# MLP kernel on one core: tile 1's last four blocks turned by DVE, tile 2's late cells moved behind rows 4 to 7's first piece, two centring steps on Pool

## The chip, the cores and the metric

The kernel runs on one core of a Trainium2 chip, in one launch. The metric is the device time in microseconds (us). Unless another thing is said, times inside the kernel are counted from the start of the profiled execution's span.

## The reference

The input x has 2048 tokens of 1024 channels, in bf16. Each token is normalized over its channels and goes through two matrix products with a gelu between.

```python
def _layernorm(x, axis=-1, eps=1e-5):
    m = jnp.mean(x, axis=axis, keepdims=True)
    v = jnp.var(x, axis=axis, keepdims=True)
    return (x - m) / jnp.sqrt(v + eps)

def reference(x, w1, b1, w2, b2):              # x (1, 2048, 1024), w1 (1024, 3584), w2 (3584, 1024)
    y = _layernorm(x, axis=-1)
    h = _gelu(jnp.einsum("bsd,df->bsf", y, w1) + b1)
    return jnp.einsum("bsf,fd->bsd", h, w2) + b2
```

## The kernel before

**Tiling.** A tile is 128 tokens, a block of tokens is four tiles (512), and there are four blocks. A row is 128 of the 3584 columns of w1, so there are 28 rows. For the first product TensorE needs tokens transposed, with channels on the partitions: `yT_sb`, eight channel blocks of 128 (index `dt`, or `j`). A full matmul takes one row and one channel block against 512 tokens. Per block of tokens, the 28 rows of the first product (eight matmuls each, `mm1_row`, L370) go through gelu on ScalarE (ACT, L396) into `hT_sb`; then the second product runs over 28 row blocks for each of four tiles and two halves of the output (`out_chunk`, L438), VectorE (DVE) adds b2 (L449), and SP stores.

**The start of block 0.** While the weights are still arriving, TensorE already works. Tiles 0, 1 and 2 (`RAW`) enter the first product untouched, as raw x, and the normalization is applied afterwards to the sums. Rows 0 to 7 (the wave) are cut into cells: a cell is one row and one channel block for some of the tiles (`wave_cell`, `pe_wave`, L386). w1 for these rows comes in pieces of 128 or 256 KB (`PIECES`): rows 0 to 3 with channel blocks 0, 1, 2-3, 4-5, 6-7 (loads w0 to w4), then rows 4 to 7 with blocks 0-1, 2-3, 4-5, 6-7 (w5 to w8). The tiles of x are loads x0 to x3. SP issues the loads in the order of `SP_FIRST_LOADS` (b1 and w0 go through ACT's queue).

**How raw tiles are turned.** TensorE transposes a 128 x 128 block into PSUM (`pe_T_one`, L331), and ACT copies it from there (`put_copy`, L343). For channel blocks 4 to 7 of tile 2 it is done in another way: DVE transposes 32 x 32 squares within each quarter of the partitions into `xq_sb` (`turn_2`, L492), and 16 small copies put the squares in their places, eight on Pool (L505) and eight on ACT (L509). Their events are `tup2` and `tua2`. Tile 3 is normalized on DVE first (L268) and turned in the same manner, whole (L479, moves at L484, L487, L516).

**Statistics.** DVE makes the statistics of a tile (L254, L264), Pool raises the variance to the power -1/2 (L261, event `rstd<i>`). DVE turns means and powers of tiles 0 to 2 into rows (L469), ACT spreads them over the partitions (L475) as `row_b(0)` and `row_b(1)`.

**Fixes and centring.** For rows 0 to 7 the raw sums are mended by DVE in PSUM: L545 subtracts the mean times the column sum of w1, L548 multiplies by the power; then gelu. Rows 8 to 27 of block 0 use centred tokens instead: four centring steps (`ops_centre`, L538, events `ctr0` to `ctr3`) subtract the mean row from `yT_sb`, two channel blocks and three tiles in each step (128 x 768 elements), into the second buffer of `yT_sb`. Row 8's matmul of channel block `dt` waits for step `dt // 2`. Their power is multiplied in PSUM (L412).

**What sets the order.** Each engine runs a list that the program writes out by hand; waits are on named events. The part of DVE's list that matters here is

```python
seq = st[0] + st[1][:1] + turn_2() + st[1][1:] + st[2] + turn_m[:2] + st[3] + turn_m[2:] + nm[3] + moves_3() + turn_r + ctr[:2]
...
for o in [a0, a1, b0, b1_] + ctr[2:] + [o for f in fixes[2:] for o in f]:
```

where `a0, b0, a1, b1_` are the fixes of rows 0 and 1. Pool's list is: the power of tile 0, tile 2's eight moves, the powers of tiles 1, 2 and 3, tile 3's moves. TensorE's list in the start is: transposes of tiles 0 and 1; cells of w0 for tile 0, then tile 1; four transposes of tile 2; then w1 for tiles 0 and 1; w0 and w1 for tile 2; w2 for all three; w3 for tiles 0 and 1, then tile 2; and from w4 on all three tiles in each cell (386 columns with two columns of ones that give the column sums). Then tile 3 for rows 0 to 7 (128 columns each), then row 8 and on.

Of the kernel before, what the change touches and what calls it, by code (L numbers as in the profile page):

```python
# [9 lines left out]
I32 = mybir.dt.int32  # L10

LN_EPS = 1e-5
P = 128
# [7 lines left out]
RAW = (0, 1, 2)  # L21
N_WARM = 25
GROUPS = (0, 2, 8)
# [3 lines left out]
N_AHEAD = 6  # L27
N_EARLY = 1
N_PAIR = 3
N_TURN = 4  # L30
POOL_TURNS = tuple((tq, (tq + k) % 4) for k in (1, 2) for tq in range(4))
CENTRE = (0, 2, 4, 6, 8)
DVE_MOVES = ((0, 0), (1, 1), (2, 2))
POOL_MOVES = ((3, 3), (0, 1), (1, 2), (2, 3), (0, 2), (1, 3))
W1_COLS = (512, 1024, 1024)
N_W2_CHUNKS = 4
SP_FIRST_LOADS = ("b1", "x0", "x1", "w0", "x2", "w1", "w2", "w3", "x3", "w4", "w5", "w6", "w7", "w8")
N_ONES = 2
PAD = 64

# [56 lines left out]
def bass_standalone__mixer_channel_mlp__prompt_kernel(  # L97
# [13 lines left out]
    DT = D // P  # L111
# [35 lines left out]
    with ExitStack() as es:  # L147
# [178 lines left out]
        def pe_T_one(i, groups, banks, j):  # L326
            k = next(n for n, g in enumerate(groups[1:]) if j < g)
            first, last = j == groups[k], j + 1 == groups[k + 1]
            waits = ["ident", x_ev[i][0]] + ([bank_read[banks[k]]] if banks[k] in bank_read else []) if first else []
            o = (j - groups[k]) * P  # L330
            pe.op(lambda e: e.transpose(out=bank_of[banks[k]][:, o:o + P], in_=x_sb[:, i, j * P:(j + 1) * P],  # L331
                                        identity=ident[:, :]), waits=waits, sig=(f"tp{i}_{k}" if last else None))
            yT_ev.setdefault(i, [None] * DT)[j] = f"te{i}_{k}"
            pe_t[0] += 0.056

        def put_copy(i, groups, banks, k):
            g0, g1 = groups[k:k + 2]
            bname = banks[k]
            assert banks.count(bname) == 1
            src = bank_of[bname][:, 0:(g1 - g0) * P].bitcast(I32)  # L340
            src = src.rearrange("p (j s) -> p j s", j=g1 - g0)
            dst = yT_sb[:, 0, g0:g1, ycol(i):ycol(i) + P].bitcast(I32)
            act.op(lambda e, dst=dst, src=src: e.copy(out=dst, in_=src), waits=[f"tp{i}_{k}"], sig=f"te{i}_{k}")  # L343
            bank_read[bname] = f"te{i}_{k}"
# [32 lines left out]
        def pe_wave(r, dt, tiles, bank, waits, sig):  # L377
            raw = tiles[0] == 0
            base = raw_at if tiles[0] in RAW else 0
            y0 = ycol(tiles[0]) - (N_ONES if raw else 0)  # L380
            n0 = base + y0 - ycol(RAW[0]) if tiles[0] in RAW else 0
            n1 = n0 + ycol(tiles[-1]) + P - y0
            w = list(waits) + (["onecols"] if raw else []) + [yT_ev[t][dt] for t in tiles]
            w += ["tup2"] if 2 in tiles and dt >= N_TURN else []
            w.append(f"w1c{w1_chunk_of(r, dt)}")
            pe.op(lambda e: e.matmul(  # L386
                unit_bank(bank)[:, n0:n1], lhsT=w1_sb[:, dt, r * P:(r + 1) * P], rhs=yT_sb[:, 0 if tiles[0] in RAW else ybuf(0), dt, y0:y0 + n1 - n0],
                start=(dt == 0 and tiles[0] in (0, 3)), stop=(dt == DT - 1), skip_group_check=True),
                waits=w, sig=sig)
            pe_t[0] += _mm_us(n1 - n0)  # L390
            if sig:
                est[sig] = pe_t[0]
# [80 lines left out]
        def put_row_spread(k, q0, q1):  # L473
            for q in range(q0, q1):
                act.op(lambda e, q=q: e.copy(out=row_b(k)[32 * q:32 * (q + 1)], in_=row_b(k)[0:32]),  # L475
                       waits=[f"row_q{k}"], sig=(f"row_{k}" if q == 3 else None))

        def moves_3():
            res = [(lambda e: e.transpose(out=xq_sb[:, :], in_=x_sb[:, 3, :]), [y_ev[3][-1], "tua2", "tup2"], "xq", 1.07)]  # L479
            for tq, q in POOL_MOVES + DVE_MOVES:  # L480
                src = xq_sb[32 * tq:32 * (tq + 1), :].rearrange("p (j q s) -> p j q s", j=DT, q=4)[:, :, q, :].bitcast(I32)
                dst = yT_sb[32 * q:32 * (q + 1), ybuf(0), :, ycol(3) + 32 * tq:ycol(3) + 32 * (tq + 1)].bitcast(I32)
                if (tq, q) in POOL_MOVES:
                    pool.op(lambda e, src=src, dst=dst: e.tensor_copy(out=dst, in_=src), waits=["xq"],  # L484
                            sig=("tg3" if (tq, q) == POOL_MOVES[-1] else None))
                if (tq, q) in DVE_MOVES:
                    res.append((lambda e, src=src, dst=dst: e.tensor_copy(out=dst, in_=src), ["xq"],  # L487
                                ("tc3" if len(res) == len(DVE_MOVES) else None), 0.2))
            return res

        def turn_2():
            return [(lambda e: e.transpose(out=xq_sb[:, 0:(DT - N_TURN) * P], in_=x_sb[:, 2, N_TURN * P:]),  # L492
                     [x_ev[2][0]], "xq2", 0.64)]

        def put_moves_2(eng):
            todo = POOL_TURNS
            if eng is act:
                todo = [m for m in ((tq, q) for tq in range(4) for q in range(4)) if m not in POOL_TURNS]
            for n, (tq, q) in enumerate(todo):
                src = xq_sb[32 * tq:32 * (tq + 1), 0:(DT - N_TURN) * P]  # L500
                src = src.rearrange("p (j q s) -> p j q s", j=DT - N_TURN, q=4)[:, :, q, :].bitcast(I32)
                dst = yT_sb[32 * q:32 * (q + 1), 0, N_TURN:DT, ycol(2) + 32 * tq:ycol(2) + 32 * (tq + 1)].bitcast(I32)
                sig = "tup2" if eng is pool else "tua2"
                if eng is pool:
                    pool.op(lambda e, src=src, dst=dst: e.tensor_copy(out=dst, in_=src),  # L505
                            waits=["xq2"] + {0: ["rstd0"], 4: ["tup2_0"]}.get(n, []),
                            sig={3: "tup2_0", 7: sig}.get(n))
                else:
                    act.op(lambda e, src=src, dst=dst: e.copy(out=dst, in_=src), waits=["xq2"], sig=(sig if n + 1 == len(todo) else None))  # L509

        def put_moves_3():
            todo = [(tq, q) for tq in range(4) for q in range(4) if (tq, q) not in DVE_MOVES + POOL_MOVES]
# [36 lines left out]
                     [f"fx_a{r}", "row_1"], f"fx_b{r}", 0.42)]  # L549

        st = {0: [op_stats(0, 0), op_stats(0, 1), op_aggr(0)]}
        put_moves_2(pool)
        st.update({i: [op_stats(i, 0), op_stats(i, 1), op_aggr(i)] for i in range(1, TPB)})
        nm = {3: ops_norm(3)}
        turn_m, turn_r = ops_row_turn(0), ops_row_turn(1)
        ctr = ops_centre()
        seq = st[0] + st[1][:1] + turn_2() + st[1][1:] + st[2] + turn_m[:2] + st[3] + turn_m[2:] + nm[3] + moves_3() + turn_r + ctr[:2]
        for o in seq:
            dve_put(o)

        pe_b1()
        put_b1()
        T_BANKS = (("t", "2_0"), ("2_1", "1_4"), ("t", "2_0"))
        for t, j in [(0, j) for j in range(N_AHEAD)] + [(1, j) for j in range(GROUPS[1])] + [
                (0, j) for j in range(N_AHEAD, DT)] + [(1, j) for j in range(GROUPS[1], DT)]:
            pe_T_one(t, GROUPS, T_BANKS[t], j)
        for k in range(2):
            for t in RAW[:2]:
                put_copy(t, GROUPS, T_BANKS[t], k)
        wave = [new_unit() for _ in range(R)]  # L570
        opened = set()

        def wave_cell(r, dt, tiles, sig=None):
            waits = [] if r in opened else wave[r][1]
            opened.add(r)
            pe_wave(r, dt, tiles, wave[r][0], waits, sig)

        cells_of = lambda a, b: [(r, dt) for j0, j1, rows in PIECES[a:b] for dt in range(j0, j1) for r in rows]
        for t in RAW[:2]:
            for r, dt in cells_of(0, N_EARLY):  # L580
                wave_cell(r, dt, (t,))
        G2 = (0, GROUPS[1], N_TURN)
        for j in range(N_TURN):
            pe_T_one(2, G2, T_BANKS[2], j)
        for k in range(2):
            put_copy(2, G2, T_BANKS[2], k)
        put_moves_2(act)
        for j in range(N_TURN, DT):
            yT_ev[2][j] = "tua2"
        put_row_spread(0, 1, 4)  # L590
        for r, dt in cells_of(N_EARLY, N_PAIR - 1):
            wave_cell(r, dt, RAW[:2])
        for r, dt in cells_of(0, N_PAIR - 1):
            wave_cell(r, dt, RAW[2:])
        for r, dt in cells_of(N_PAIR - 1, N_PAIR):
            wave_cell(r, dt, RAW)
        for r, dt in cells_of(N_PAIR, N_PAIR + 1):
            wave_cell(r, dt, RAW[:2])
        for r, dt in cells_of(N_PAIR, N_PAIR + 1):
            wave_cell(r, dt, RAW[2:])  # L600
        cells = cells_of(N_PAIR + 1, len(PIECES))
        for n, (r, dt) in enumerate(cells):
            wave_cell(r, dt, RAW, f"raw_{r}" if dt == DT - 1 else None)
        cs_ev = {}

        def put_cs(c0, c1, src):
# [3 lines left out]
            for r in mine:  # L610
                cs_ev[r] = f"cs{c0}"

        put_cs(0, 4, ps_1[:, 0:4, one0:one0 + 1])
        put_moves_3()
        put_row_spread(1, 1, 3)
# [10 lines left out]
            act_gelu(r, 0, TPB, wave[r][0], f"fx_b{r}", f"g_0_{r}")  # L626
            hT_row[(0, r)] = f"g_0_{r}"
        (a0, b0), (a1, b1_) = fixes[:2]
        for o in [a0, a1, b0, b1_] + ctr[2:] + [o for f in fixes[2:] for o in f]:
            dve_put(o)  # L630
        for t in RAW:
            yT_ev[t] = [f"ctr{k}" for k, (j0, j1) in enumerate(zip(CENTRE[:-1], CENTRE[1:])) for _ in range(j0, j1)]
# [94 lines left out]
```

## Time and profile before

| | us |
|---|---|
| median of 3 runs (lowest, highest) | 396.15 (395.9, 396.18) |
| profiled execution | 396.51 |
| its span, first to last instruction | 395.3 |

The profiled execution's time holds 1.2 us around its span. The granted clock of TensorE is 1.00. In the lines that follow, PE is TensorE's matmul and PEld its weight load, and a name such as L386 is the line of the kernel. A line of the timeline has start, length, engine, line, operation, out<-in, shape and count; several instructions of one kind are merged, so that the length covers all of them, and matmuls overlap each other in their pipeline. A line that begins with a source line gives the shortest, median and longest duration in ns and the first and last start.

### The profile page before, as it was taken

The page shows a single profiled execution, that of the slowest core. Times are in us where ns is not written, and L with a number is a line of the kernel's source. Part 1 is how long each engine was busy: PE and PEld are TensorE (multiplying, and loading weights), DVE is VectorE, ACT ScalarE, POOL GpSimd, SP SyncE. Part 2 cuts the span into 40 slices and gives each one's busy share as a digit, 9 for nine tenths or more (in the row PEclk, how much of TensorE's full clock was granted, in tenths as well). Part 3 has the DMA queues.
Part 4 walks back from the last instruction along what each step waited for, and adds up shares of the span by engine and source line. Part 5 has one row for each costly group of instructions (what it writes and reads, how often), then busy time and mean ns, then how long its engine had stood idle before and what let it go on. Part 6 is the DMA issues. An engine that isn't in the chain of part 4 may idle for free.

```text
span 395.3 us, 4562 instructions
## 1 busy us (share of the span) xinstructions
PE 390.9 (99%) x1916; PEld 185.8 (47%) x1950; DVE 162.7 (41%) x339; ACT 87.1 (22%) x145; POOL 14.0 (4%) x69
## 2 busy tenths in 40 slices
PE   9999999999999999999999999999999999999998
PEld 8744444444444444444444444444444444444444
DVE  6998889998999306987100000001100000001011
ACT  5655420000134332000023443000003334400000
POOL 5201000011001100000000000000000000000000
PEclk9999999999999999999999999999999999999999
DMA  7999930000000000000000000000000000000000
GB/s 273 375 385 387 387 139 27 15 27 14 28 0 0 2 0 0 28 27 15 27 13 2 0 0 2 13 13 28 25 15 15 0 2 0 0 15 27 13 28 27
DMA packets 16078, 23.63 MB, mean 60 GB/s; under 512 B 1082, under 2 KB 8250, under 8 KB 16058
## 3 DMA queue, kind: packets, MB, share of 16 engines
q1 hardware_dynamic: 15872, 23.20, 16.5%
q8 instruction: 15, 0.25, 0.3%
q10 hardware_dynamic: 186, 0.14, 0.1%
q14 instruction: 5, 0.04, 0.0%
HBM read 19.14 MB, written 4.19 MB: 59 GB/s over the span
## 4 chain that ended last, share of the span: by engine, by line
PE 99%; issue 0%; DVE 0%
PE ps L438 49%; PE ps L370 38%; PE ps_t L370 7%; PE ps L386 3%; PE ps L460 1%; PE ps_t L386 0%; PE ps L331 0%; PE ps_t L331 0%; DVE o_sb L449 0%; PE ps L521 0%
## 5 line engine op out<-in xcount | busy, mean ns | idle before, releaser
L438 PE MATMUL ps<-w_sb,hT_sb 128*128 128x512 bf16 (+2 forms) x909 | 193.3, 373 | 0.8
L370 PE MATMUL ps<-yT_sb,w_sb 128*128 128x512 bf16 x678 | 152.4, 379 | 0.9
L438 PEld LDWEIGHTS ps<-w_sb,hT_sb 128*128 128x128 bf16 x924 | 88.6, 98 | 105.2
L396 ACT ACTIVATE hT_sb<-ps,b_sb 128x512 bf16<-128x512 f32 x94 | 64.0, 688 | 234.9 <-PE ps L370 217.2
L370 PEld LDWEIGHTS ps<-yT_sb,w_sb 128*128 128x128 bf16 x696 | 68.1, 98 | 81.9
L449 DVE TENSOR_TENSOR o_sb<-ps,b_sb 128x512 bf16<-128x512 f32 (+2 forms) x33 | 22.3, 676 | 198.7 <-PE ps L438 198.5
L310 DVE STREAM_TRANSPOSE yT_sb<-x_sb 32x256 bf16<-32x256 bf16 x192 | 83.7, 436 | 21.9 <-PE ps_t L370 18.8
L370 PE MATMUL ps_t<-yT_sb,w_sb 128*128 128x512 bf16 x135 | 31.9, 379 | 0.1
L254 DVE BATCH_NORM_STATS2 st_sb<-x_sb 128x6 f32<-128x512 bf16 x32 | 21.1, 671 | 3.5 <-DMA x_sb<-in_x_dram 3.4
L370 PEld LDWEIGHTS ps_t<-yT_sb,w_sb 128*128 128x128 bf16 x136 | 13.3, 98 | 16.1
L396 ACT ACTIVATE hT_sb<-ps_t,b_sb 128x512 bf16<-128x512 f32 x18 | 12.4, 687 | 17.1 <-PE ps_t L370 14.6
L386 PE MATMUL ps<-yT_sb,w_sb 128*128 128x128 bf16 (+3 forms) x132 | 14.4, 262 | 0.0
L386 PEld LDWEIGHTS ps<-yT_sb,w_sb 128*128 128x128 bf16 x132 | 10.0, 101 | 2.8
L261 POOL TENSOR_TENSOR rstd_sb<-mv_sb,nhalf 128x1 f32<-128x1 f32 x13 | 7.1, 548 | 111.7 <-DVE mv_sb L264 111.7
L412 DVE TENSOR_TENSOR ps<-ps,row_r 128x384 f32<-128x384 f32 x17 | 9.2, 563 | 3.1 <-PE ps L370 2.8
L268 DVE TENSOR_SCALAR x_sb<-x_sb,mv_sb,rstd_sb 128x1024 bf16<-128x1024 bf16 x13 | 7.0, 541 | 2.0 <-POOL rstd_sb L261 1.3
L545 DVE SCALAR_TENSOR_TENSOR ps<-row_r,ncs,ps 128x384 f32<-128x384 f32 x7 | 4.2, 614 | 0.5 <-PE ps L386 0.5
L548 DVE TENSOR_TENSOR ps<-ps,row_r 128x384 f32<-128x384 f32 x7 | 3.9, 563 | 0.2
L538 DVE TENSOR_TENSOR yT_sb<-yT_sb,row_r 128x768 bf16<-128x768 bf16 x4 | 3.6, 952 | 0.0
L460 PE MATMUL ps<-const-bfloat16-1.0 128*128 128x128 bf16 x25 | 2.8, 312 | 0.8 <-PEq L712 0.8
L475 ACT COPY row_r<-row_r 32x384 f32<-32x384 f32 x6 | 3.1, 509 | 2.2 <-DVE row_r L469 2.1
L386 PE MATMUL ps_t<-yT_sb,w_sb 128*128 128x386 bf16 (+1 forms) x16 | 3.2, 273 | 0.0
(37 smaller groups left out, 36.9 us busy)
## 6 DMA issues: line engine op xcount, KB each, us to landing
w_sb<-in_w_dram SPq DMA_DIRECT2D x4, 1792.0 KB, 18.3
w_sb<-in_w_dram SPq DMA_DIRECT2D x2, 2048.0 KB, 15.8
out_dram<-o_sb SPq DMA_DIRECT2D x31, 128.0 KB, 1.7
x_sb<-in_x_dram SPq DMA_DIRECT2D x3, 1024.0 KB, 14.5
w_sb<-in_w_dram SPq DMA_DIRECT2D x7, 256.0 KB, 5.5
x_sb<-in_x_dram SPq DMA_DIRECT2D x4, 256.0 KB, 3.3
w_sb<-in_w_dram SPq DMA_DIRECT2D x1, 1024.0 KB, 9.3
b_sb<-in_b_dram SPq DMA_DIRECT2D x1, 256.0 KB, 14.4
```

Of the source, the lines that this page charges most:

```text
L254: return (lambda e, i=i, h=h, pw=pw: e.bn_stats(st_sb[i][:, 6 * h:6 * (h + 1)], x_sb[:, i, h * pw:(h + 1) * pw]), [x_ev[i][h if len(x_ev[i ...
L261: pool.op(lambda e, i=i, dst=dst, mv=mv: e.tensor_tensor(out=dst, in0=mv[:, 1:2], in1=nhalf[:, i:i + 1], op=ALU.pow), waits=[f"mv{i}", "nh ...
L268: return (lambda e, i=i, c0=c0, c1=c1: e.tensor_scalar(out=x_sb[:, i, c0:c1], in0=x_sb[:, i, c0:c1], scalar1=mv_sb[:, i, 0:1], scalar2=rst ...
L310: res.append((lambda e, src=src, dst=dst: e.transpose(out=dst, in_=src), waits, (f"tr{i}" if lastop else None), 0.47))
L370: pe.op(lambda e, b=b, r=r, dt=dt, bank=bank: e.matmul(unit_bank(bank)[:, 0:TB], lhsT=w1_sb[:, dt, r * P:(r + 1) * P], rhs=yT_sb[:, ybuf(b ...
L386: pe.op(lambda e: e.matmul(unit_bank(bank)[:, n0:n1], lhsT=w1_sb[:, dt, r * P:(r + 1) * P], rhs=yT_sb[:, 0 if tiles[0] in RAW else ybuf(0) ...
L396: act.op(lambda e, r=r, n0=n0, n1=n1, bank=bank: e.activation(out=hT_sb[:, r, n0:n1], in_=unit_bank(bank)[:, n0:n1], func=ACT.Gelu_apprx_tanh,
L412: crit.append((est[sig], (lambda e, reg=reg: e.tensor_tensor(out=reg, in0=reg, in1=row_b(1), op=ALU.mult), [sig, "row_1"], ready, 0.57), 0))
L438: pe.op(lambda e, sl=sl, ft=ft, c0=c0, c1=c1, bank=bank: e.matmul(ps_2[:, bank, 0:c1 - c0], lhsT=hT_sb[:, ft, sl * P:(sl + 1) * P], rhs=w2 ...
L449: crit.append((est[sig], (lambda e, ob=ob, c0=c0, c1=c1, bank=bank: e.tensor_tensor(out=o_sb[:, ob, c0:c1], in0=ps_2[:, bank, 0:c1 - c0], ...
L460: pe.op(lambda e: e.matmul(ps_1[:, 0, 0:P], lhsT=ones, rhs=ones, start=True, stop=True))
L545: return [(lambda e: e.scalar_tensor_tensor(out=reg, in0=row_b(0), scalar=ncs[:, c:c + 1], in1=reg, op0=ALU.mult, op1=ALU.add), [f"m1_0_{r ...
```

## The change

- `TURNED = (1, 2)`: channel blocks 4 to 7 of tile 1 are turned as those of tile 2 were. TensorE makes four transposes fewer, ACT's second copy of tile 1 shrinks from six blocks to two, DVE transposes once more, Pool and ACT make eight moves more each. DVE's list has both turns behind the statistics of tile 0. ACT makes four of tile 1's moves ahead of tile 2's copies from PSUM, the rest behind. Pool makes tile 1's moves, then tile 2's, ahead of the powers of tiles 1 to 3. Pool's moves of a tile wait for the moves ahead of them.
- The cells of rows 0 to 3 with channel blocks 4 to 7 (w3 and w4) run for tiles 0 and 1 first, then come rows 4 to 7 with blocks 0 and 1 (w5) for all three tiles, and then the same late cells for tile 2.
- w4 is loaded ahead of x3.
- `POOL_CENTRE = (2, 3)`: Pool makes the centring steps `ctr2` and `ctr3`, behind tile 3's moves and `ctr0`. DVE makes `ctr0` ahead of the fixes and `ctr1` behind those of rows 0 and 1.

```diff
@@ -30,11 +30,13 @@
 N_TURN = 4
 POOL_TURNS = tuple((tq, (tq + k) % 4) for k in (1, 2) for tq in range(4))
 CENTRE = (0, 2, 4, 6, 8)
+POOL_CENTRE = (2, 3)
+TURNED = (1, 2)
 DVE_MOVES = ((0, 0), (1, 1), (2, 2))
 POOL_MOVES = ((3, 3), (0, 1), (1, 2), (2, 3), (0, 2), (1, 3))
 W1_COLS = (512, 1024, 1024)
 N_W2_CHUNKS = 4
-SP_FIRST_LOADS = ("b1", "x0", "x1", "w0", "x2", "w1", "w2", "w3", "x3", "w4", "w5", "w6", "w7", "w8")
+SP_FIRST_LOADS = ("b1", "x0", "x1", "w0", "x2", "w1", "w2", "w3", "w4", "x3", "w5", "w6", "w7", "w8")
 N_ONES = 2
 PAD = 64
 
@@ -381,7 +383,7 @@
             n0 = base + y0 - ycol(RAW[0]) if tiles[0] in RAW else 0
             n1 = n0 + ycol(tiles[-1]) + P - y0
             w = list(waits) + (["onecols"] if raw else []) + [yT_ev[t][dt] for t in tiles]
-            w += ["tup2"] if 2 in tiles and dt >= N_TURN else []
+            w += [f"tup{t}" for t in TURNED if t in tiles and dt >= N_TURN]
             w.append(f"w1c{w1_chunk_of(r, dt)}")
             pe.op(lambda e: e.matmul(
                 unit_bank(bank)[:, n0:n1], lhsT=w1_sb[:, dt, r * P:(r + 1) * P], rhs=yT_sb[:, 0 if tiles[0] in RAW else ybuf(0), dt, y0:y0 + n1 - n0],
@@ -476,7 +478,7 @@
                        waits=[f"row_q{k}"], sig=(f"row_{k}" if q == 3 else None))
 
         def moves_3():
-            res = [(lambda e: e.transpose(out=xq_sb[:, :], in_=x_sb[:, 3, :]), [y_ev[3][-1], "tua2", "tup2"], "xq", 1.07)]
+            res = [(lambda e: e.transpose(out=xq_sb[:, :], in_=x_sb[:, 3, :]), [y_ev[3][-1]] + [f"tu{e}{t}" for e in "ap" for t in TURNED], "xq", 1.07)]
             for tq, q in POOL_MOVES + DVE_MOVES:
                 src = xq_sb[32 * tq:32 * (tq + 1), :].rearrange("p (j q s) -> p j q s", j=DT, q=4)[:, :, q, :].bitcast(I32)
                 dst = yT_sb[32 * q:32 * (q + 1), ybuf(0), :, ycol(3) + 32 * tq:ycol(3) + 32 * (tq + 1)].bitcast(I32)
@@ -488,25 +490,29 @@
                                 ("tc3" if len(res) == len(DVE_MOVES) else None), 0.2))
             return res
 
-        def turn_2():
-            return [(lambda e: e.transpose(out=xq_sb[:, 0:(DT - N_TURN) * P], in_=x_sb[:, 2, N_TURN * P:]),
-                     [x_ev[2][0]], "xq2", 0.64)]
-
-        def put_moves_2(eng):
+        HX = (DT - N_TURN) * P
+        xq_of = lambda i: xq_sb[:, (i - TURNED[0]) * HX:(i - TURNED[0] + 1) * HX]
+
+        def turn_half(i):
+            return [(lambda e: e.transpose(out=xq_of(i), in_=x_sb[:, i, N_TURN * P:]), [x_ev[i][0]], f"xq{i}", 0.64)]
+
+        def moves_half(eng, i):
             todo = POOL_TURNS
             if eng is act:
                 todo = [m for m in ((tq, q) for tq in range(4) for q in range(4)) if m not in POOL_TURNS]
             for n, (tq, q) in enumerate(todo):
-                src = xq_sb[32 * tq:32 * (tq + 1), 0:(DT - N_TURN) * P]
+                src = xq_of(i)[32 * tq:32 * (tq + 1), :]
                 src = src.rearrange("p (j q s) -> p j q s", j=DT - N_TURN, q=4)[:, :, q, :].bitcast(I32)
-                dst = yT_sb[32 * q:32 * (q + 1), 0, N_TURN:DT, ycol(2) + 32 * tq:ycol(2) + 32 * (tq + 1)].bitcast(I32)
-                sig = "tup2" if eng is pool else "tua2"
+                dst = yT_sb[32 * q:32 * (q + 1), 0, N_TURN:DT, ycol(i) + 32 * tq:ycol(i) + 32 * (tq + 1)].bitcast(I32)
                 if eng is pool:
+                    first = "rstd0" if i == TURNED[0] else f"tup{i - 1}"
                     pool.op(lambda e, src=src, dst=dst: e.tensor_copy(out=dst, in_=src),
-                            waits=["xq2"] + {0: ["rstd0"], 4: ["tup2_0"]}.get(n, []),
-                            sig={3: "tup2_0", 7: sig}.get(n))
+                            waits=[f"xq{i}"] + {0: [first], 4: [f"tup{i}_0"]}.get(n, []),
+                            sig={3: f"tup{i}_0", 7: f"tup{i}"}.get(n))
                 else:
-                    act.op(lambda e, src=src, dst=dst: e.copy(out=dst, in_=src), waits=["xq2"], sig=(sig if n + 1 == len(todo) else None))
+                    act.op(lambda e, src=src, dst=dst: e.copy(out=dst, in_=src), waits=[f"xq{i}"],
+                           sig=(f"tua{i}" if n + 1 == len(todo) else None))
+                yield
 
         def put_moves_3():
             todo = [(tq, q) for tq in range(4) for q in range(4) if (tq, q) not in DVE_MOVES + POOL_MOVES]
@@ -549,24 +555,30 @@
                      [f"fx_a{r}", "row_1"], f"fx_b{r}", 0.42)]
 
         st = {0: [op_stats(0, 0), op_stats(0, 1), op_aggr(0)]}
-        put_moves_2(pool)
+        for t in TURNED:
+            for _ in moves_half(pool, t):
+                pass
         st.update({i: [op_stats(i, 0), op_stats(i, 1), op_aggr(i)] for i in range(1, TPB)})
         nm = {3: ops_norm(3)}
         turn_m, turn_r = ops_row_turn(0), ops_row_turn(1)
         ctr = ops_centre()
-        seq = st[0] + st[1][:1] + turn_2() + st[1][1:] + st[2] + turn_m[:2] + st[3] + turn_m[2:] + nm[3] + moves_3() + turn_r + ctr[:2]
+        seq = st[0] + turn_half(1) + turn_half(2) + st[1] + st[2] + turn_m[:2] + st[3] + turn_m[2:] + nm[3] + moves_3() + turn_r + ctr[:1]
         for o in seq:
             dve_put(o)
 
         pe_b1()
         put_b1()
         T_BANKS = (("t", "2_0"), ("2_1", "1_4"), ("t", "2_0"))
-        for t, j in [(0, j) for j in range(N_AHEAD)] + [(1, j) for j in range(GROUPS[1])] + [
-                (0, j) for j in range(N_AHEAD, DT)] + [(1, j) for j in range(GROUPS[1], DT)]:
-            pe_T_one(t, GROUPS, T_BANKS[t], j)
+        GH = (0, GROUPS[1], N_TURN)
+        for t, j in [(0, j) for j in range(N_AHEAD)] + [(1, j) for j in range(GH[1])] + [
+                (0, j) for j in range(N_AHEAD, DT)] + [(1, j) for j in range(GH[1], N_TURN)]:
+            pe_T_one(t, GROUPS if t == 0 else GH, T_BANKS[t], j)
         for k in range(2):
             for t in RAW[:2]:
-                put_copy(t, GROUPS, T_BANKS[t], k)
+                put_copy(t, GROUPS if t == 0 else GH, T_BANKS[t], k)
+        act_moves = [m for t in TURNED for m in (moves_half(act, t),)]
+        for _ in range(4):
+            next(act_moves[0])
         wave = [new_unit() for _ in range(R)]
         opened = set()
 
@@ -579,28 +591,33 @@
         for t in RAW[:2]:
             for r, dt in cells_of(0, N_EARLY):
                 wave_cell(r, dt, (t,))
-        G2 = (0, GROUPS[1], N_TURN)
         for j in range(N_TURN):
-            pe_T_one(2, G2, T_BANKS[2], j)
+            pe_T_one(2, GH, T_BANKS[2], j)
         for k in range(2):
-            put_copy(2, G2, T_BANKS[2], k)
-        put_moves_2(act)
-        for j in range(N_TURN, DT):
-            yT_ev[2][j] = "tua2"
+            put_copy(2, GH, T_BANKS[2], k)
+        for m in act_moves:
+            for _ in m:
+                pass
+        for t in TURNED:
+            for j in range(N_TURN, DT):
+                yT_ev[t][j] = f"tua{t}"
         put_row_spread(0, 1, 4)
+        done = lambda r, dt: f"raw_{r}" if dt == DT - 1 else None
+        late = [c for c in cells_of(0, len(PIECES)) if c[0] < PIECES[0][2][-1] + 1 and c[1] >= N_TURN]
         for r, dt in cells_of(N_EARLY, N_PAIR - 1):
             wave_cell(r, dt, RAW[:2])
         for r, dt in cells_of(0, N_PAIR - 1):
             wave_cell(r, dt, RAW[2:])
         for r, dt in cells_of(N_PAIR - 1, N_PAIR):
             wave_cell(r, dt, RAW)
-        for r, dt in cells_of(N_PAIR, N_PAIR + 1):
+        for r, dt in late:
             wave_cell(r, dt, RAW[:2])
-        for r, dt in cells_of(N_PAIR, N_PAIR + 1):
-            wave_cell(r, dt, RAW[2:])
-        cells = cells_of(N_PAIR + 1, len(PIECES))
-        for n, (r, dt) in enumerate(cells):
-            wave_cell(r, dt, RAW, f"raw_{r}" if dt == DT - 1 else None)
+        for r, dt in cells_of(N_PAIR + 2, N_PAIR + 3):
+            wave_cell(r, dt, RAW)
+        for r, dt in late:
+            wave_cell(r, dt, RAW[2:], done(r, dt))
+        for r, dt in cells_of(N_PAIR + 3, len(PIECES)):
+            wave_cell(r, dt, RAW, done(r, dt))
         cs_ev = {}
 
         def put_cs(c0, c1, src):
@@ -610,6 +627,8 @@
             for r in mine:
                 cs_ev[r] = f"cs{c0}"
 
+        for k in POOL_CENTRE:
+            pool.op(ctr[k][0], waits=ctr[k][1] + ["tg3", "ctr0"], sig=ctr[k][2])
         put_cs(0, 4, ps_1[:, 0:4, one0:one0 + 1])
         put_moves_3()
         put_row_spread(1, 1, 3)
@@ -626,7 +645,7 @@
             act_gelu(r, 0, TPB, wave[r][0], f"fx_b{r}", f"g_0_{r}")
             hT_row[(0, r)] = f"g_0_{r}"
         (a0, b0), (a1, b1_) = fixes[:2]
-        for o in [a0, a1, b0, b1_] + ctr[2:] + [o for f in fixes[2:] for o in f]:
+        for o in [a0, a1, b0, b1_] + ctr[1:POOL_CENTRE[0]] + [o for f in fixes[2:] for o in f]:
             dve_put(o)
         for t in RAW:
             yT_ev[t] = [f"ctr{k}" for k, (j0, j1) in enumerate(zip(CENTRE[:-1], CENTRE[1:])) for _ in range(j0, j1)]
```

## The prediction

> **What bounds the kernel now.** I read the page's busy times first, then the chain of waits, then the timeline from 0 to 60 us, because the change touches only the first 21 us.
>
> ```profile
> span 395.3 us, 4562 instructions
> ...
> PE 390.9 (99%) x1916; PEld 185.8 (47%) x1950; DVE 162.7 (41%) x339; ACT 87.1 (22%) x145; POOL 14.0 (4%) x69
> ...
> PE 99%; issue 0%; DVE 0%
> ```
>
> TensorE has work all the time, and the chain that ended last is TensorE from end to end. So only two things can move the end: the columns that TensorE has to stream, and a wait that opens a hole in its stream. All other engines count only through the second. The timeline gives the price of a column, and the times of those who feed TensorE (start, length, operation):
>
> ```profile
> 3.90 1.70 PE L331 MATMUL ps<-ident,x_sb 128*128 128x128 bf16 x14
> ...
> 4.89 0.64 DVE L254 BATCH_NORM_STATS2 st_sb<-x_sb 128x6 f32<-128x512 bf16 x1
> ...
> 5.45 0.69 DVE L492 STREAM_TRANSPOSE xq_sb<-x_sb 128x512 bf16<-128x512 bf16 x1
> ...
> 6.20 2.15 POOL L505 COPY yT_sb<-xq_sb 32x64 int32<-32x64 int32 x8 [0.58 <-DVE xq_sb L492]
> ...
> 7.03 2.01 ACT L509 COPY yT_sb<-xq_sb 32x64 int32<-32x64 int32 x8
> ...
> 10.58 0.55 POOL L261 TENSOR_TENSOR rstd_sb<-mv_sb,nhalf 128x1 f32<-128x1 f32 x1 [1.03 <-DVE mv_sb L264]
> ...
> 11.17 0.55 DVE L268 TENSOR_SCALAR x_sb<-x_sb,mv_sb,rstd_sb 128x1024 bf16<-128x1024 bf16 x1
> ...
> 13.06 1.99 POOL L484 COPY yT_sb<-xq_sb 32x128 int32<-32x128 int32 x6 [1.93 <-DVE xq_sb L479]
> ...
> 14.97 1.83 DVE L538 TENSOR_TENSOR yT_sb<-yT_sb,row_r 128x768 bf16<-128x768 bf16 x2
> ...
> 16.70 3.29 PE L386 MATMUL ps<-yT_sb,w_sb 128*128 128x128 bf16 x56
> ...
> 19.34 1.81 DVE L538 TENSOR_TENSOR yT_sb<-yT_sb,row_r 128x768 bf16<-128x768 bf16 x2
> ...
> 20.49 8.58 PE L370 MATMUL ps<-yT_sb,w_sb 128*128 128x512 bf16 x39
> ```
>
> The 14 transposes start (1.70-0.31)/13 = 0.107 us apart; the 56 matmuls of the same 128 columns at 16.70 start (3.29-0.22)/55 = 0.056 apart. Before about 6.6 us TensorE runs at half speed, after that at full speed, and it never pauses between. By the same reckoning 258 columns take 0.110 and 386 take 0.163 at full speed.
>
> **TensorE's columns.** Tile 1 loses four transposes. They stood in the slow stretch at 0.107, but the stretch ends at a time, as far as this trace tells: cells that now come earlier fill it. So they are worth 4 x 0.056 = -0.22 us. If it ended after a count of matmuls, they would be worth 4 x 0.107 = -0.43. The Trainium skill (TensorE: Matmul & The Clock Gate, § Part 1: The HAM clock gate) says that the warm-up budget is time and not a number of matmuls; by that -0.22 stands, and one trace can't show it. Against it, 16 cells (rows 0 to 3, blocks 4 to 7) are now split by tile, where 8 were: 8 x (0.110 + 0.056 - 0.163) = +0.02. Columns: -0.20.
>
> **Tile 1's blocks 4 to 7, and ACT ahead of tile 2's copy.** DVE's added transposition (0.69) takes 4.89 to 5.58. ACT then makes four of tile 1's moves before tile 2's first copy out of PSUM: 4 x 0.25 from 5.62 to 6.63, so that copy (0.27 long, started 6.72 before) ends at 6.90, and TensorE can use it at about 6.97. TensorE gets there sooner now: the first cells move from 5.40 to 4.97, eight of them at 0.107 reach 5.83, tile 2's transposes 6.26, and four 258-column cells across the change of speed 6.87. That is a hole of 0.1 us; it could be 0 to 0.2, as no hand-over from ACT to TensorE ends a wait in this trace. I take +0.10.
>
> The blocks themselves: Pool's eight moves run from about 5.7 (after its first power, 5.06 + 0.55) to 7.9, ACT's last four to 8.0. TensorE asks for them at 6.97 + 8 x 0.056 + 8 x 0.163 = 8.7. The cover is 0.7 us, so nothing.
>
> **The moved cells and the two loads.** The late cells of tiles 0 and 1 run from 8.7 to 10.5 (16 x 0.110). Their loads, by the view of the DMAs: the third piece lands at 7.8, w4, now in x3's place, at about 8.5, for cells that need it at 9.6. Rows 4 to 7's first piece (w5) lands at 10.1 as before, is used at 10.5 instead of 11.5, and has 0.4 us left. Tile 2's late cells at 11.8 need Pool's second eight moves (to about 10.2) and ACT's eight (to 10.1). x3 lands at about 9.2; DVE's statistics of tile 3, pushed from 8.96 by the added transposition (0.61 with its overlap), start at 9.57. SP issues these loads back to back with no wait between, so only these two change places. Nothing; each cover is named.
>
> **Pool's queue.** Behind Pool's eight added moves (2.2 us) stand the three powers. Tile 3's moves from 10.58 to about 11.35, because the two others are ahead of it. DVE's normalization of tile 3 waits for it: 11.17 becomes about 11.9. All that follows (turn, moves on three engines, first centring step) is 0.75 later, and ACT's last move of tile 3 ends at 15.9 instead of 15.2. TensorE asks for tile 3 at about 16.6 (16.70 - 0.20 + 0.10). The cover is 0.7 us: nothing, but this is the thinnest chain.
>
> **The centring steps.** Before, DVE made two of them ahead of the row fixes and two behind. Now it makes the first, ending near 16.7; Pool, which waits for that one, makes the third and fourth; DVE makes the second behind the first four fix instructions, from about 19.3. TensorE opens row 8 at 20.27 - 0.10 = 20.2 and needs the second step at its third matmul, 20.2 + 2 x 0.216 = 20.6, the third at 21.05, the fourth at 21.5.
>
> What a step costs on Pool the trace does not show. Nearest rows: Pool's copies of 64 and of 128 elements.
>
> ```profile
> L505 POOL COPY yT_sb<-xq_sb x8: 226/229/232, 6.2 to 8.1; 32x64 int32<-32x64 int32 x8
> ...
> L484 POOL COPY yT_sb<-xq_sb x6: 285/288/342, 13.1 to 14.8; 32x128 int32<-32x128 int32 x6
> ...
> L487 DVE COPY yT_sb<-xq_sb x3: 216/221/314, 13.0 to 13.5; 32x128 int32<-32x128 int32 x3
> ```
>
> 59 ns for 64 elements more is 0.92 ns an element, over a fixed 0.17 (0.21 with the pause between two). 768 elements cost 0.9 us if two inputs go like one, and 0.21 + 2 x 768 x 0.92 ns = 1.6 us if they go one after the other. With the 0.55 of the power, the only two-input operation of Pool here, as fixed part, it is 1.95. I take 1.6, since it is a two-input operation with little to compute, and keep 0.9 and 1.95. (GPSIMD Engine Reference, § 3.1, of the Trainium skill has 4497 ns for a two-input add of 2048 elements, an estimate of 1.7 us for 768; by it the sum below would be 0.2 higher.)
>
> So Pool is busy from 16.8 to 18.4 and to 20.0, within its own two dates (21.05, 21.5). But DVE's second step wants to start at 19.3, in the middle of it. The rows show what happens when DVE and Pool read SBUF together: of DVE's three equal copies at 13.0 to 13.8, beside Pool's moves, one took 314 ns and not 216 to 221, and one of Pool's 342 and not 288. The 0.1 lost is about the element part of one Pool copy (128 x 0.92 = 0.12), as if one had stood aside until the other's elements were through. On that reading DVE's step waits for Pool's to finish: 20.0 + 0.95 = 20.95, with two hand-overs 21.0. TensorE stands 0.4 us at row 8's third matmul. If Pool's step costs 0.9 the wait is 0; at 1.95 it is 1.1.
>
> The Trainium skill (SBUF — State Buffer, § Who interferes with whom) says that a DVE instruction with two SBUF inputs and a Pool instruction that reads SBUF exclude each other for the whole instruction; this is the rule that speaks against the change. Taken by the 0.1 of the rows alone the sum would be 0.4 lower; the trace has no two-input DVE step beside a long Pool one.
>
> **The sum:** -0.20 + 0.10 + 0.41 = +0.31 us. The profiled execution took 396.51 with a span of 395.3, and would take 396.8; it lay 0.36 above the median of 396.15. On the median: 396.5. A measurement of this kernel can tell about 0.2% (0.8 us) from no change, so the forecast is: no change that can be told.
>
> **The rivals.**
> - *No clash (27%).* DVE and Pool run side by side, or Pool's step takes under 1.2 us. For it: the first centring step started while Pool's last move was ending, and all four took 948 to 958 ns. Against: that meeting was 0.07 us long, and the copies did lose 0.1. The sum is -0.10: 396.05.
> - *Pool's step is long, and DVE's waits for it (33%): slower.* The same mechanism from the point where a step costs over 1.85 us: then TensorE's hole is above 0.9 and the sum above +0.8. At 1.95: 16.8 + 3.9 = 20.7, DVE done at 21.7, hole 1.1, sum +1.0, 397.15; at 2.3 DVE is done at 22.4, sum +1.7, 397.85. For it: Pool's only two-input rows have 0.55 where a copy has 0.2, and the step mixes types and repeats a row. Against: those rows are powers.
> - *Tile 3 comes late (2%): slower.* If Pool's 16 moves cost over 0.7 us more than 16 x 0.27, TensorE waits at 16.6; another 1 us would give 397.4.
> - *The four transposes are worth more (2%).* To be faster by 0.8 us would take more than the -0.43 of the slow price and no hole, so something that I don't see.
> - The forecast itself has 36%.
>
> **How the numbers follow.** Within 0.2%: forecast and no clash, 36 + 27 = 63%; slower 33 + 2 = 35%; faster 2%. The range goes from no hole at all (-0.20, 395.95, less 0.1 of scatter) to a Pool step of 2.2 us (397.7); the forecast's own range is 396.0 to 396.9.
>
> **What would show it.** In the profile after: L331's group with 16 matmuls and not 20; Pool's two TENSOR_TENSOR of 768 elements and their length (0.9, 1.6 or 1.95); the second centring step on DVE starting late or lasting over 0.95 while Pool is in its fourth; the 512-column matmuls of row 8 starting with a pause after the second; a start at 20.2 of that row if the early steps are right, and later if tile 3 was late. I am wrong on the main point if that DVE step lasts 0.95 beside a busy Pool, and wrong altogether if the pause is elsewhere.

## The result, and the profile after

Median of 12 runs 397.0 us (396.88 to 397.15), beside 396.12 of the kernel before in the same comparison (395.81 to 396.3): ratio 1.0023, 95% interval 1.0014 to 1.0032. That is +0.88 us, 0.23% slower. The forecast was 396.5, no change that can be told. The measurement was finer than the forecast took it to be: its interval does not reach 1, and the ratio lies just on the other side of the 0.2% bound. The forecast's own range (396.0 to 396.9) missed the time by 0.1. Only the wide range held it, whose upper end was there for a long Pool step, and that is not what happened.

The page of the kernel after, the same lines as were read before:

```profile
span 395.9 us, 4624 instructions
...
PE 392.1 (99%) x1954; PEld 184.7 (47%) x1954; DVE 162.6 (41%) x338; ACT 88.7 (22%) x153; POOL 19.1 (5%) x79
...
PE 97%; DVE 1%; DMA 1%; ACT 0%; issue 0%
```

The chain that ended last is no longer TensorE alone: DVE, a load and ACT are in it. The view of the waits, for TensorE, names the three holes (before, TensorE had none of them; the idle time shown is less than the hole, since a matmul's modelled end overlaps the next start):

```profile
PE ps_t L333 <- DMA x_sb<-in_x_dram: 0.6, 1, 0.6
PE ps L372 <- DVE yT_sb L544: 0.4, 1, 0.4
PE ps L388 <- ACT yT_sb L345: 0.2, 1, 0.2
```

The second is the one that was forecast, and the timeline shows it from each side (L544 is the centring step, L551 and L554 the fixes, L372 the 512-column matmuls):

```profile
16.06 0.96 DVE L544 TENSOR_TENSOR yT_sb<-yT_sb,row_r 128x768 bf16<-128x768 bf16 x1
17.40 1.15 DVE L551 SCALAR_TENSOR_TENSOR ps<-row_r,ncs,ps 128x384 f32<-128x384 f32 x2 [0.38 <-PE ps L388]
18.45 1.02 DVE L554 TENSOR_TENSOR ps<-ps,row_r 128x384 f32<-128x384 f32 x2
19.39 1.88 DVE L544 TENSOR_TENSOR yT_sb<-yT_sb,row_r 128x768 bf16<-128x768 bf16 x1
...
17.19 3.26 POOL L544 TENSOR_TENSOR yT_sb<-yT_sb,row_r 128x768 bf16<-128x768 bf16 x2 [1.07 <-DVE yT_sb L544]
...
20.32 0.59 PE L372 MATMUL ps<-yT_sb,w_sb 128*128 128x512 bf16 x2
21.32 0.60 PE L372 MATMUL ps<-yT_sb,w_sb 128*128 128x512 bf16 x2 [0.40 <-DVE yT_sb L544]
```

DVE's second step begins at 19.39 and lasts 1.88 instead of 0.96. Pool is at its two steps until 17.19 + 3.26 = 20.45; DVE's ends 0.82 later, at 21.27. TensorE has done two matmuls of row 8 and starts the third at 21.32, where 20.32 + 2 x 0.216 = 20.75 was its own time: a hole of 0.57 us.

The other two holes come before 8 us, and they show something that the profile before had hidden:

```profile
5.94 0.28 PE L333 MATMUL ps_t<-ident,x_sb 128*128 128x128 bf16 x2 [0.59 <-DMA x_sb<-in_x_dram]
...
6.29 0.61 PE L388 MATMUL ps<-yT_sb,w_sb 128*128 128x258 bf16 x4
7.11 0.29 PE L388 MATMUL ps<-yT_sb,w_sb 128*128 128x128 bf16 x2 [0.21 <-ACT yT_sb L345]
...
5.77 1.01 ACT L513 COPY yT_sb<-xq_sb 32x64 int32<-32x64 int32 x4 [0.32 <-DVE xq_sb L497]
6.79 0.27 ACT L345 COPY yT_sb<-ps_t 128x128 int32<-128x128 int32 x1
```

In this execution TensorE's slow phase ended near 4.0 us and not near 6.6, so it came to tile 2's transposes at 5.18, before x2 had landed (a hole of 0.75, until 5.94), and to tile 2's first cells at about 6.74, before ACT, behind four moves, had copied them: a hole of 0.37 there.

### The profile page after: what moved, and what is told of

The parts are those of the page before. It is cut to its first block, busy times and chain, and to the rows that moved or that the text cites. A ratio compares the mean times of both kernels' runs of the same rounds, so it can differ in the third digit from the quotient of the medians.

```text
span 395.9 us, 4624 instructions
## 1 busy us (share of the span) xinstructions
PE 392.1 (99%) x1954; PEld 184.7 (47%) x1954; DVE 162.6 (41%) x338; ACT 88.7 (22%) x153; POOL 19.1 (5%) x79
## 4 chain that ended last, share of the span: by engine, by line
PE 97%; DVE 1%; DMA 1%; ACT 0%; issue 0%
PE ps L440 49%; PE ps L372 38%; PE ps_t L372 7%; PE ps L388 2%; DMA x_sb<-in_x_dram 1%; DVE yT_sb L544 0%; PE ps_t L388 0%; DVE ps L554 0%; ACT yT_sb L513 0%; DVE ps L551 0%; DVE st_sb L256 0%; DVE xq_sb L497 0%; ACT yT_sb L345 0%; DVE o_sb L451 0%; DVE stat_r L266 0%
## 5 line engine op out<-in xcount | busy, mean ns | idle before, releaser
L372 PE MATMUL ps<-yT_sb,w_sb 128*128 128x512 bf16 x696 | 153.7, 379 | 0.4 <-DVE yT_sb L544 0.4
L372 PEld LDWEIGHTS ps<-yT_sb,w_sb 128*128 128x128 bf16 x696 | 68.0, 98 | 82.6 <-DVE yT_sb L544 0.9
L372 PE MATMUL ps_t<-yT_sb,w_sb 128*128 128x512 bf16 x136 | 32.1, 379 | 0.0
L372 PEld LDWEIGHTS ps_t<-yT_sb,w_sb 128*128 128x128 bf16 x136 | 13.3, 98 | 16.0
L551 DVE SCALAR_TENSOR_TENSOR ps<-row_r,ncs,ps 128x384 f32<-128x384 f32 x7 | 4.2, 613 | 0.4 <-PE ps L388 0.4
L513 ACT COPY yT_sb<-xq_sb 32x64 int32<-32x64 int32 x16 | 3.9, 242 | 0.5 <-DVE xq_sb L497 0.3
L554 DVE TENSOR_TENSOR ps<-ps,row_r 128x384 f32<-128x384 f32 x7 | 3.9, 564 | 0.2
L509 POOL COPY yT_sb<-xq_sb 32x64 int32<-32x64 int32 x16 | 3.7, 230 | 0.9
```

The source lines that it names most:

```text
L372: pe.op(lambda e, b=b, r=r, dt=dt, bank=bank: e.matmul(unit_bank(bank)[:, 0:TB], lhsT=w1_sb[:, dt, r * P:(r + 1) * P], rhs=yT_sb[:, ybuf(b ...
L551: return [(lambda e: e.scalar_tensor_tensor(out=reg, in0=row_b(0), scalar=ncs[:, c:c + 1], in1=reg, op0=ALU.mult, op1=ALU.add), [f"m1_0_{r ...
```

## The experiments

Two theories stood against each other. *Clash*: the loss is the hole at row 8, and DVE's second centring step is late because Pool's steps exclude it. *Early part*: the loss lies before row 8, in ACT's list or the loads. Each comparison below has 11 runs of the kernel and 21 or 33 of the kernel before, whose median was 396.18 to 396.27. It was 396.12 beside the changed kernel, so 0.15 us between two comparisons says nothing by itself.

**All centring on DVE.**

```diff
-POOL_CENTRE = (2, 3)
+POOL_CENTRE = ()
-... + moves_3() + turn_r + ctr[:1]
+... + moves_3() + turn_r + ctr[:2]
-for o in [a0, a1, b0, b1_] + ctr[1:POOL_CENTRE[0]] + ...
+for o in [a0, a1, b0, b1_] + ctr[2:] + ...
```

> The changed kernel with its centring put back on DVE: steps 1 and 2 ahead of the row fixes, 3 and 4 behind those of rows 0 and 1, none on Pool; all else as changed. Theory (clash): the changed kernel's hole of 0.57 us at row 8's third matmul comes from DVE's second step standing aside for Pool's; it is gone here, each centring step on DVE takes 0.95, and the time is 397.0 - 0.57 = 396.45. Rival (early part): the loss of 0.88 between the medians lies mostly before row 8, in the four moves ahead of tile 2's copy; then 0.3 to 0.6 stays and the time is 396.5 to 396.7. Rival (the hole has another cause, such as the DVE chain being 1.1 us later): the hole stays, at another matmul of row 8, and the time is 396.9 to 397.1.

Measured: 396.52 us (396.48 to 396.89), ratio to before 1.0006 (0.9997 to 1.0014). All four steps take 0.95 to 0.96, and TensorE has no hole:

```profile
L544 DVE TENSOR_TENSOR yT_sb<-yT_sb,row_r x4: 947/950/958, 15.8 to 20.4; 128x768 bf16<-128x768 bf16 x4
```

Taking Pool's steps away is worth about half a microsecond, and the expected 396.45 was met within 0.1. But 396.52 is also the lower end of what the early part was to leave, 396.5 to 396.7, so the time alone does not choose; that the hole is gone does. About 0.25 above the kernel before stays.

**Only the centring change, on the kernel before.**

```diff
-seq = ... + turn_r + ctr[:2]
+seq = ... + turn_r + ctr[:1]
-for o in [a0, a1, b0, b1_] + ctr[2:] + ...
+for o in [a0, a1, b0, b1_] + ctr[1:2] + ...
+for k in (2, 3):
+    pool.op(ctr[k][0], waits=ctr[k][1] + ["tg3", "ctr0"], sig=ctr[k][2])
```

> The kernel before with only the centring change: Pool makes steps 3 and 4 behind tile 3's moves and step 1, DVE makes step 2 behind the fixes of rows 0 and 1. Theory (clash, a matter of when): without the added turn the first step ends at 15.9 and not 17.0, so Pool is at its two steps from 16.1 to 19.35 and DVE's second step at 19.35 hardly meets it; no hole, the time is that of before, within 0.1. Rival (the two steps cost their hole wherever they stand): 0.5 to 0.6 slower than before. Rival (Pool's steps hold up the row fixes too, which read SBUF as well): the fixes last over 0.62 and 0.56, and the time is 0.3 or more above before.

Measured: 396.55 us (396.4 to 396.96), ratio 1.0006 (0.9997 to 1.0015). My expectation that the two would not meet was a miss. Its timeline:

```profile
16.65 3.27 POOL L538 TENSOR_TENSOR yT_sb<-yT_sb,row_r 128x768 bf16<-128x768 bf16 x2 [1.40 <-ACT ncs L608]
...
18.73 2.00 DVE L538 TENSOR_TENSOR yT_sb<-yT_sb,row_r 128x768 bf16<-128x768 bf16 x1
...
20.79 0.60 PE L370 MATMUL ps<-yT_sb,w_sb 128*128 128x512 bf16 x2 [0.53 <-DVE yT_sb L538]
```

Pool began half a microsecond after the first step had ended (16.14), for a reason that I did not settle, and in this execution TensorE, quick early, let DVE come to its second step at 18.73 and not at 19.35. So the clash is there without tile 1's turn: the step lasts 2.00, the hole is 0.69. But everything stands 0.5 earlier, the third matmul at 20.79 instead of 21.32, and so the time is 0.45 less than with the whole change. In time alone this run does not tell from before.

**One step on Pool.** The edit is `POOL_CENTRE = (3,)`; DVE makes steps 2 and 3 behind the first fixes.

> The changed kernel with one step only on Pool, the fourth; DVE makes steps 2 and 3 behind the fixes of rows 0 and 1. Theory (clash): Pool is at its step from 17.2 to 18.85, before DVE comes to its second step at 19.4; no clash, no hole (step 2 ends at 20.25 for 20.75, step 3 at 21.1 for 21.2, which is tight: up to 0.1), time 396.45 as with all steps on DVE. Rival (any step on Pool costs): a hole of 0.2 to 0.5 stays, 396.7 to 397.0.

Measured: 396.53 us (396.44 to 396.73). Pool's step runs from 16.89 for 1.65, DVE's two from 19.21 for 1.81 together, at their own length. TensorE waits 0.07 us for the second of them and for nothing else at row 8. A step on Pool does no harm if DVE does not meet it.

**DVE's second step first.** Ahead of the fixes instead of behind; Pool as in the change.

```diff
-... + moves_3() + turn_r + ctr[:1]
+... + moves_3() + turn_r + ctr[:2]
-for o in [a0, a1, b0, b1_] + ctr[1:POOL_CENTRE[0]] + ...
+for o in [a0, a1, b0, b1_] + ...
```

> The changed kernel with DVE's second step ahead of the row fixes, right behind the first; Pool still makes steps 3 and 4. Theory (clash; who starts first has the other wait until its end): DVE's second step starts at 16.95 and takes 0.95, Pool's third step asks for SBUF at 17.2 and waits until about 17.9, so its row lasts about 2.3 instead of 1.65, and the fourth ends at 21.1, before TensorE's need at 21.6; no hole, time 396.45. Rival (they share the port and slow each other): DVE's step lasts 1.3 or more and Pool's about 2; the fixes start later, and up to 0.3 of hole stays, 396.5 to 396.8.

Measured: 396.49 us (396.38 to 396.68). This is the test of how the two exclude each other. The answer for the centring line (shortest, median, longest of the steps on each engine), after and here:

```profile
L544 DVE TENSOR_TENSOR yT_sb<-yT_sb,row_r x2: 959/1420/1881, 16.1 to 19.4; 128x768 bf16<-128x768 bf16 x2
L544 POOL TENSOR_TENSOR yT_sb<-yT_sb,row_r x2: 1642/1647/1652, 17.2 to 18.8; 128x768 bf16<-128x768 bf16 x2
```

```profile
L544 DVE TENSOR_TENSOR yT_sb<-yT_sb,row_r x2: 950/954/959, 15.8 to 16.7; 128x768 bf16<-128x768 bf16 x2
L544 POOL TENSOR_TENSOR yT_sb<-yT_sb,row_r x2: 1645/1926/2206, 17.0 to 19.1; 128x768 bf16<-128x768 bf16 x2
```

Whoever starts first runs at its own length, 950 or 1645, and the other's row is stretched by the wait. They do not share: neither runs at half pace. DVE's step after ends 0.82 us after Pool's, Pool's step here ends 1.51 after DVE's (19.16 after 17.65), so each does all but some 0.13 us of its own work once the other is through. The two other profiles in which DVE met a running Pool step say the same: 1.88, 2.00 and 2.08 long, DVE's step ended 0.81 to 0.82 after Pool's each time. DVE's fixes, with one input in PSUM, are not touched by a busy Pool (L551 609 to 622 ns after, 611 to 617 with no step on Pool).

**Two of tile 1's moves ahead of tile 2's copies, not four** (on the kernel with one step on Pool).

```diff
-for _ in range(4):
+for _ in range(2):
     next(act_moves[0])
```

> The kernel with one centring step on Pool (the fourth), and ACT makes two of tile 1's moves ahead of tile 2's copies from PSUM, not four. Theory: with the clash gone, what is left of the loss (about 0.25 against before) is TensorE's hole at tile 2's first cells, which wait for ACT's copy behind four moves: 0.9 us in the profile where TensorE's slow phase ended at 3.3 us, 0.4 where it ended at 4.0, none where it ended at 6.7. Two moves fewer ahead let the copy start 0.5 earlier: the hole is at most 0.5 in any profile, the third piece of w1 (landing 6.7 to 7.0) becomes the next limit, and the time is 396.1 to 396.3. Rival (the early part is bound by the landing of x2 and w2 whatever ACT does): 396.5 as before this edit. Rival (the moves left behind come late for tile 1's late cells): a hole at the first 258-column cell behind the 386-column ones, 396.5 or more.

Measured: 396.32 us (396.18 to 396.55, and one run at 398.22); beside 396.53 with four, 0.2 less. Against before the two figures disagree: the medians are 0.05 us apart, the ratio is 1.0009 (0.9999 to 1.0018). By neither does this kernel tell from before. With four ahead, the profile (slow phase until about 3.6 us) has the hole at tile 2's first cells with 0.73 of idle time behind ACT's copy:

```profile
5.58 0.61 PE L388 MATMUL ps<-yT_sb,w_sb 128*128 128x258 bf16 x4
6.93 0.45 PE L388 MATMUL ps<-yT_sb,w_sb 128*128 128x128 bf16 x5 [0.73 <-ACT yT_sb L345]
```

With two ahead it is gone. What stays in that profile is a wait at the very first cells, as w0 landed at 5.4 there, and 0.2 us in row 8 for DVE's third centring step.

**None ahead.** The loop of the last edit is left out.

> The same with none of tile 1's moves ahead of tile 2's copies. Theory: the hole at tile 2's first cells is gone in every profile (TensorE waits there for loads only), but ACT sits idle until tile 2's transposes are done, so the eight moves end at 8.2 to 9.2, and where the slow phase ends late TensorE waits up to 0.5 us at tile 1's late cells (asked for at 8.3 to 8.6): 396.2 to 396.6. Rival (ACT's order does not matter): 396.5, with the hole where it was.

Measured: 396.38 us (396.21 to 396.86), within the expected span. The slow phase of the profiled execution ended at 5.0, so the hole that was foreseen for a late end could not be seen. TensorE is early enough there to find w5 not yet landed (10.26): the 0.4 us that covered this load before are used up, and 0.24 us of idle time stand before rows 4 to 7's first piece.

**Order of cells and loads alone, on the kernel before.** `late` cells and `"w4", "x3"` as in the change, nothing else.

> The kernel before with only the order of the cells and of the loads w4 and x3 changed; tile 1 turned by TensorE, all centring on DVE. Theory: eight more split cells cost 0.02 us, all covers hold (w5 lands at 10.1 for a use at 10.5), so the time is that of before, within 0.1 (396.2 to 396.4 beside 396.27). Rival (order or loads cost something): 0.25 slower, which would then explain the kernels with all centring on DVE. A profile with a hole at rows 4 to 7's first piece (near 10.3) speaks for the loads.

Measured: 396.2 us (396.02 to 396.74), ratio 0.9998 (0.9989 to 1.0007): no change, as expected.

**x3 ahead of w4 again** (on the kernel with one step on Pool).

> The kernel with one centring step on Pool, with x3 loaded ahead of w4 as before the change. Theory: neither load is waited for in any profile (tile 3's statistics start near 10.0 behind other DVE work, w4's cells near 9.7), so nothing changes: 396.5 as without this edit. Rival: w4 comes late for its cells near 9.7 and makes a hole of up to 0.2, 396.6 to 396.7; or x3's earlier landing lets DVE's chain run earlier and saves 0.1 or more.

Measured: 396.58 us (396.52 to 396.75), beside 396.53: no change. This kernel, with four moves ahead, was measured in the same comparison as those with two and none, so it is the nearest measure of what the moves cost: 396.32 and 396.38 against 396.58.

**The change with two moves ahead, the clash left in.** The same edit of the loop, on the kernel after.

> The changed kernel, Pool making steps 3 and 4 as there, with two of tile 1's moves ahead of tile 2's copies and not four. Theory (the later wait swallows the earlier): the end of DVE's second step is set by DVE's and Pool's chain, not by TensorE; TensorE reaches row 8 some 0.2 to 0.4 earlier and its hole at the third matmul grows by the same, to 0.6 to 1.0. Time 396.95 to 397.05, as without this edit. Rival (the two losses add): 396.75, 0.25 less, as this edit gave where there was no clash.

Measured: 397.01 us (396.95 to 397.24), ratio 1.0022 (1.0013 to 1.0031): the edit that gave 0.2 elsewhere gives nothing here. TensorE opens row 8 about 0.4 earlier, and its hole grows from 0.57 to 0.91:

```profile
20.11 0.38 PE L372 MATMUL ps<-yT_sb,w_sb 128*128 128x512 bf16 x1
21.24 0.61 PE L372 MATMUL ps<-yT_sb,w_sb 128*128 128x512 bf16 x2 [0.75 <-DVE yT_sb L544]
```

**All centring on DVE, two moves ahead.**

> All centring on DVE and two of tile 1's moves ahead: what is left of the change is tile 1's turn, the order of the cells and of the loads. Theory: like the kernel with one step on Pool and two moves ahead, 396.2 to 396.4; Pool's single step neither gains nor costs. Against before (396.27) the four transposes less show at most as 0.2, and only where the slow phase ends late, so the two can hardly be told apart. Rival (Pool's step relieved DVE): 396.5.

Measured: 396.58 us (396.53 to 396.73), ratio 1.0009 (1.0000 to 1.0018). The expectation missed, and the time is the rival's: 0.26 more than with the fourth step on Pool. The two kernels were measured in different comparisons, and their ratios to before are the same, 1.0009, so the gain of Pool's single step rests on the profile more than on the times. With two steps ahead of the fixes on a DVE that is already late by the added turn, everything that DVE has to deliver for row 8 is late. The timeline of DVE and of TensorE's weight loads (PEld; a matmul waits with its weight load):

```profile
17.75 1.14 DVE L551 SCALAR_TENSOR_TENSOR ps<-row_r,ncs,ps 128x384 f32<-128x384 f32 x2
...
20.60 0.95 DVE L544 TENSOR_TENSOR yT_sb<-yT_sb,row_r 128x768 bf16<-128x768 bf16 x1
...
20.14 0.98 PEld L372 LDWEIGHTS ps<-yT_sb,w_sb 128*128 128x128 bf16 x6 [0.23 <-ACT hT_sb L398]
21.61 0.33 PEld L372 LDWEIGHTS ps<-yT_sb,w_sb 128*128 128x128 bf16 x3 [0.49 <-DVE yT_sb L544]
```

The fixes start at 17.75, so row 0's gelu, whose bank row 8 needs, ends only just before 20.14; and the fourth step ends at 21.55, for a matmul that would have started some 0.1 to 0.2 sooner. So with all centring on DVE it is, by this profile, DVE's list and not ACT's moves that keeps the time above before.

## Why the prediction was right in its mechanism, and what was mis-sized

From row 8's third matmul to the last one's start the kernel takes 372.57 to 372.58 us before (20.70 to 393.27) and after (21.32 to 393.90). So the end is decided at that matmul.

- **The centring steps.** Pool's step was put at 1.6 us; it takes 1.65, and two start 1.62 apart. That they stand in DVE's way, taken from 0.1 us in three copies, was right. The Trainium skill (SBUF — State Buffer, § Who interferes with whom) has it that the two exclude each other for the whole instruction; the rows of both orders agree, but for the 0.13 us. The hole was put at 0.41 and is 0.57.
- **What mis-sized it is Pool's start.** I had the first step end at 16.7 and Pool start at 16.8; they were at 17.02 and 17.19. So Pool's two steps ended at 20.45 and not at 20.0; DVE's step then ended 0.82 and not 0.95 after them, which gave 0.13 back, and row 8's third matmul started at 21.32 where I had 21.0. Behind the late start is DVE's normalization of tile 3, 1.08 later (12.25 instead of 11.17), where I had 0.75. I had let Pool's queue alone set it. In fact DVE's statistics of tile 3 began at 10.04 and not at 9.57, and DVE and Pool's queue were ready for the last power together, at 11.6. In this execution DVE had its first data 0.19 later, and the second turn waited 0.18 for x2:

```profile
5.08 0.65 DVE L497 STREAM_TRANSPOSE xq_sb<-x_sb 128x512 bf16<-128x512 bf16 x1
5.92 0.71 DVE L497 STREAM_TRANSPOSE xq_sb<-x_sb 128x512 bf16<-128x512 bf16 x1 [0.18 <-DMA x_sb<-in_x_dram]
```

- **ACT ahead of tile 2's copy** was put at +0.10, 0 to 0.2. It is 0.37 in the profile after, and 0.9 in the one with the slow phase ending at about 3.6. I had worked it out for the one execution shown, where TensorE was slow until 6.6.
- **The columns** were put at -0.20, on the same ground. No kernel here shows a gain over before. Where the slow phase ends early, TensorE waits for x2 or w2 soon after, and columns ahead of a load's landing are worth nothing. Of the changed kernels only the one with all centring on DVE was profiled with a late end (6.7): it has no hole, and its row 8 opens at 20.20, 0.07 ahead of before.
- **The sum hides a maximum.** The hole of 0.41 was counted from row 8's own moved opening, so -0.20 + 0.10 + 0.41 is no more than 21.0 against the 20.70 of before, and the two early terms drop out of it. The kernel behaves so while the clash is there: row 8's third matmul is released by DVE and Pool, and what TensorE does earlier does not show. Two moves ahead gave 0.2 without the clash and nothing with it. So the two early terms, both mis-sized, did not shift the forecast by their errors; that they did not was luck. It also fits the spread: 0.27 us from lowest to highest after, where the 12 runs of before beside it spread over 0.49 and 33 later ones over 1.2 (395.67 to 396.83).
- **The base.** The profiled execution of before, 396.51, stood 0.24 to 0.39 above the medians of the later comparisons. I noted the distance to the median and did not ask where it came from. The kernel with the order alone changed takes the time of before and opens row 8 at 20.08 in its profile, with a slow phase until 5.0; the profile of before, slow until 6.6, opened it at 20.27. So a late slow phase is the likely reason, and the step from 396.12 to 397.0 is larger than that from span 395.3 to 395.9. This is the second part of the miss. Execution beside execution, 396.82 was forecast and 397.15 measured, 0.33 more, which is the date of row 8's third matmul. Then I took 0.36 off for the median, as before; but the profiled execution after, though the slowest of its twelve, lies only 0.15 above its median. Where DVE and Pool set the date, a late slow phase has little left to cost, and the distance could not be carried over. The two parts, 0.33 and 0.21, are the 0.54 between 396.46 and 397.0.
- **Covers that held:** tile 1's late cells, the two loads, tile 2's late cells, tile 3 on TensorE (asked for at 16.75, ACT's last move done at 16.25). No hole is at any of them in the profile after.

Of the 0.88, the experiments give about 0.47 to the clash (397.0 to 396.53, with one step on Pool) and 0.2 to ACT's four moves ahead (396.53 to 396.32). What is left, 0.2, is mostly the 0.15 by which the median of before itself moved between the comparisons (396.12 to 396.27), and cannot be told from nothing. The split depends on the order: the centring change alone (396.55) and all the rest alone (396.52) stand 0.25 to 0.28 above before, neither of them clear of it, and together they make 0.73 to 0.88. The rival "Pool's step is long" had the size of the result, but not its cause: the step was as short as I took it. No version here beats the kernel before.

## What to carry to other kernels

A step given to Pool to relieve DVE can cost more than it saves if DVE meets it with a step that, like it, reads two inputs from SBUF: here 0.95 us became 1.9 to 2.1. Place it so that DVE meets it with operations that read PSUM, or let DVE go first. Before summing gains ahead of a wait, ask what releases the wait: if it is another chain, the gains vanish in it. And look whether the one profile at hand lies above or below the median of the runs, and which early event differs, before taking a gapless stretch for a property of the kernel.

## What was not expected of the hardware

TensorE's slow phase (0.107 us for 128 columns) ended at about 3.5, 3.6, 4.0, 4.3, 4.4, 4.8, 5.0, 6.6 and 6.7 us in profiles of kernels that begin in the same way, with its first matmul at 0.83. So it ends neither at a fixed time nor after a fixed number of matmuls. A microsecond of slow phase costs half a microsecond of work (0.107 us a matmul instead of 0.056), if no load stops TensorE first. The landing of x2, with nothing changed ahead of it, also moved, from 5.2 to 6.0 us.
